# Shifted low weight words in a PSUM tile among the up-projection's banks

## The chip, the cores and the metric

The kernel runs on one core of one Trainium2 chip. A core has five engines that work side by side: TensorE (PE; its weight loads are shown apart, as PEld), VectorE (DVE), ScalarE (ACT), GpSimd (POOL) and SyncE (SP, which here only issues transfers). SBUF is the working memory of all engines, PSUM the memory that PE writes and that DVE and ACT read and write; the kernel's operations on POOL all have their operands in SBUF. The metric is the device time of one execution in microseconds (us), the median of several runs.

## What is computed

A banded attention over 8 batches, 8 heads, 576 positions and 64 elements a head (each position sees itself and the 127 before it, with a slope per head on the distance), and after it a feed-forward network on the 4608 rows of 512 values:

```python
scores = scale * np.matmul(q, k.transpose(0, 1, 3, 2))
mask = (rel >= 0) & (rel < window)
scores = np.where(mask, scores + bias[None], -1000000000.0)
attn = softmax(scores); attn_out = np.matmul(attn, v)
x = attn_out.transpose(0, 2, 1, 3).reshape(B * S, H * D)
h = x @ w_in                                   # 512 x 2048
g = h * (1.0 / (1.0 + np.exp(-1.702 * h)))
out = (g @ w_out).astype(np.float32)           # 2048 x 512
```

The softmax is written short here. The two weight matrices reach the kernel as 64-bit words: two 32-bit words for each value, the low one first. The kernel makes fp32 values of them itself; that is the decoding that the change is about.

## The kernel before, in words

The rows of the network are worked in 18 chunks of T = 256, the hidden width in 16 slices of 128. For a chunk and a slice f, `Job.up(f)` (line 576) makes h in a PSUM tile of tag `h_ps` with 12 matmuls (the weight and the input each as a high and a low part, three products, four pieces of 128); ACT takes a tanh of it (line 585), DVE makes the gelu g from it (line 586, which reads h from PSUM too), ACT casts its high part (589) and POOL subtracts for the low part (590). `Job.down(f)` (line 593) adds 6 matmuls into two PSUM accumulators. The main loop (from line 930) emits `up` of the next step ahead of `down` of the present one. The last six chunks go in pairs, with other code (`Pair`, from 685), when all the weights have long been decoded.

Attention goes in units through a pipeline of stages, one `tick` (line 819) at a time: loads, scores on PE (line 342 in the first two batches, 352 later), bias and minimum on DVE (369), exponents on ACT (392), normalising on POOL, ACT and DVE (417, 420), transposes on PE (438), their copies (446), and the product with v (495). The first seven ticks or so run ahead of the network, with dummy matmuls between them (`spin`, 203); from then on `advance` spreads the ticks over the steps of the network.

Weights come as 32 halves, `w1` and `w2` of each of the 16 slices. `fetch` loads one as 512 64-bit words per partition into a tile of 4 KB (the loads are kept in order on SP's queue). `decode` (line 219) makes of it a high and a low fp32 part, in the same 4 KB:

- line 227, ACT: the top words, scaled, into a tile `wc` of tag `o`, of which there are five; the attention's `xb`, the network's outputs and `half`, and the tiles of `sums` use the same five.
- line 228, DVE: the low words shifted right by 29, in place.
- line 229, DVE: `wc` shifted left by 3, or-ed with those bits, into `wc`.
- line 232, ACT: the high part, a cast of `wc`; line 233, POOL: the low part, a subtraction.

`decode_next` (857) decodes the next half. Three halves are decoded during the first ticks, five at the first step of the network, about two a step until slice 7 is done, then about one a step. The first eight are pinned behind what stands ahead of them on their engine; the rest aren't. For slices from 8 on the `w1` half's `wc` is kept until its neighbour is decoded too; then `sums` (650) makes sums and differences of the pair (DVE, lines 654 to 657), casts and subtracts them (660, 661; the casts go to tiles `wh` of tag `o`) and sends them to DRAM for the paired chunks at the end (664, 665).

The order of the instructions on each engine is laid out once, when the program is built: a scheduler goes through a timeline of its own, gives each engine the first instruction in program order whose inputs are ready, and hands out a tag's buffers as tiles are first written; a buffer comes free when all readers of its tile are done. On the chip each engine then keeps this order, and waits where an input or a buffer comes later than the timeline had it. PSUM has eight banks: two for `h_ps`, one each for `s_ps` and `x_ps`, two for `t_ps` and two for the accumulators. In the first ticks the attention's products `x_ps` of the first four units also use the tag `h_ps`.

Of the kernel before, what the change touches and what calls it, by code (L numbers as in the profile page):

```python
# [11 lines left out]
I32 = mybir.dt.int32  # L12
I64 = mybir.dt.int64
AF = mybir.ActivationFunctionType
ALU = mybir.AluOpType
# [5 lines left out]
P = 128  # L21
# [132 lines left out]
def tile_kernel(ctx: ExitStack, tc: tile.TileContext, q0, k0, v0, qT, kT, v, w_in, w_out, out):  # L154
    nc = tc.nc
# [6 lines left out]
    ps = ctx.enter_context(tc.tile_pool(name="ps", bufs=1, space=PSUM))  # L162
# [56 lines left out]
    def decode(st, name, pin=lambda ins: ins):  # L219

        words = st.bitcast(I32).rearrange("p (m two) -> p m two", two=2)
        top, low = words[..., 1], words[..., 0]
        c = ffn.tile([P, 512], I32, name="wc", tag="o", bufs=OBUFS)

        pin(nc.scalar.activation(c.bitcast(F32), top.bitcast(F32), AF.Prelu, scale=2.0 ** -112, alpha=2.0 ** 32))
        pin(nc.vector.tensor_scalar(low, low, 29, None, ALU.logical_shift_right))
        pin(nc.vector.scalar_tensor_tensor(c, c, 3, low, ALU.logical_shift_left, ALU.bitwise_or))
        w = c.bitcast(F32)  # L230
        res = const.tile([P, 2, 512], F32R, name=name, tag=name)
        pin(nc.scalar.copy(res[:, 0], w))
        pin(nc.gpsimd.tensor_tensor(res[:, 1], w, res[:, 0].bitcast(F32), ALU.subtract))
        if name.startswith("w1"):
            kept[name] = w
        return res
# [620 lines left out]
    def decode_next():  # L857
        nonlocal halves
        g, ws = halves // 2, (w1, w2)[halves % 2]

        pin = [tc.keep_in_program_order] if halves < PINNED else []
        ws[g] = decode(ws[g], f"w{1 + halves % 2}_{g}", *pin)
        halves += 1
        if ws is w1 and g >= F0 and g % 2:
            sums(g // 2, kept.pop(f"w1_{g - 1}"), kept.pop(f"w1_{g}"))
# [175 lines left out]
```

## Time and profile before

| | |
|---|---|
| median of 3 runs | 1059.15 us (1058.39 to 1060.15) |
| profiled execution | 1062.32 us, span 1060.5 us |
| mean granted TensorE clock | 0.988 |
| busy share PE / PEld / DVE / ACT / POOL | 98% / 86% / 64% / 64% / 58% |
| decoding, POOL subtraction (line 233) | 32 times, 1251 ns at least, 1282 in the middle, 3418 at most |
| decoding, ACT top words (227) and cast (232) | 32 times each, 676 and 620 ns in the middle |

The profile is one execution, taken by the hardware profiler; the span runs from the first instruction to the last, and the profiled execution's own time has a little more around it. A row of a group gives line, engine, operation, the tiles written and read, the count, the busy time, the mean of one, and the idle time of the engine just before, with who ended it. A row of the timeline gives start, duration, engine, line, operation, tiles and count, and in brackets the idle time before it and its releaser. A row of the table of stages gives the stretch, its length, the busy time and count of each engine (or of one line alone), the granted clock as a share of full speed, the share of the transfer engines, and GB/s.

### The profile page before, as it was taken

The page shows a single profiled execution, that of the slowest core. Times are in us where ns is not written, and L with a number is a line of the kernel's source. Part 1 is how long each engine was busy: PE and PEld are TensorE (multiplying, and loading weights), DVE is VectorE, ACT ScalarE, POOL GpSimd, SP SyncE. Part 2 cuts the span into 40 slices and gives each one's busy share as a digit, 9 for nine tenths or more (in the row PEclk, how much of TensorE's full clock was granted, in tenths as well). Part 3 has the DMA queues.
Part 4 walks back from the last instruction along what each step waited for, and adds up shares of the span by engine and source line. Part 5 has one row for each costly group of instructions (what it writes and reads, how often), then busy time and mean ns, then how long its engine had stood idle before and what let it go on. Part 6 is the DMA issues. An engine that isn't in the chain of part 4 may idle for free.

```text
span 1060.5 us, 21877 instructions
## 1 busy us (share of the span) xinstructions
PE 1037.9 (98%) x6897; PEld 913.6 (86%) x6897; DVE 683.0 (64%) x2280; ACT 675.4 (64%) x1974; POOL 620.1 (58%) x832
## 2 busy tenths in 40 slices
PE   8889999999999999999999999999999999999998
PEld 5557878789998999999899999999988998898987
DVE  6877576357777787867778686776744345436343
ACT  6968876568777777777777777777633334335332
POOL 3668887457676677767677676766642233215121
PEclk9969999999999999999999999999999999999999
DMA  8975456333224234332423432342174556556551
GB/s 286 371 239 185 147 160 196 108 85 94 80 83 131 82 96 125 112 80 89 141 83 113 119 107 81 106 136 69 57 274 163 170 174 212 179 165 205 188 179 60
DMA packets 120276, 151.91 MB, mean 143 GB/s; under 512 B 40033, under 2 KB 96865, under 8 KB 120161
## 3 DMA queue, kind: packets, MB, share of 16 engines
q1 hardware_dynamic: 114400, 140.55, 42.6%
q10 hardware_dynamic: 5760, 9.96, 2.6%
q8 instruction: 55, 0.90, 0.4%
q14 instruction: 61, 0.49, 0.2%
HBM read 119.01 MB, written 31.46 MB: 142 GB/s over the span
## 4 chain that ended last, share of the span: by engine, by line
PE 79%; DVE 4%; issue 1%; DMA 1%; ACT 1%; POOL 0%; POOLq 0%; ACTq 0%; SPq 0%; DVEq 0%
PE acc L600 21%; PE h_ps L580 21%; PE accs L780 11%; PE X_ps L721 6%; PE s_ps L352 5%; PE x_ps L518 4%; PE Y_ps L721 4%; PE t_ps L461 4%; PE x_ps L495 1%; DVE xf L710 0%; DMA xf<-x 0%; PE t_ps L438 0%; DVE xh L564 0%; DMA part<-wc 0%; DVE xl L566 0%
## 5 line engine op out<-in xcount | busy, mean ns | idle before, releaser
L580 PE MATMUL h_ps<-xh,w 128*128 128x256 f32 x1536 | 251.5, 288 | 8.4 <-DVE g L586 7.5
L580 PEld LDWEIGHTS h_ps<-xh,w 128*128 128x128 f32 x1536 | 213.4, 190 | 26.9 <-issue 7.5
L600 PE MATMUL acc<-w,gh 128*128 128x512 f32 x768 | 220.8, 402 | 0.5 <-ACT g L585 0.4
L590 POOL TENSOR_TENSOR gl<-g,gh 128x256 fp32r<-128x256 f32 x192 | 147.1, 767 | 99.4 <-ACT gh L589 78.0
L733 POOL TENSOR_TENSOR gs<-g,gs 128x512 fp32r<-128x512 f32 x48 | 63.4, 1320 | 168.7 <-PE Y_ps L721 113.8
L780 PE MATMUL accs<-w,gs 128*128 128x512 f32 x576 | 148.3, 393 | 0.3 <-POOL gs L733 0.3
L600 PEld LDWEIGHTS acc<-w,gh 128*128 128x128 f32 x768 | 131.7, 190 | 18.2 <-ACT g L585 0.8
L330 POOL TENSOR_TENSOR K<-rk,K 128x384 fp32r<-128x384 f32 (+1 forms) x120 | 108.8, 907 | 50.7 <-ACT K L328 45.5
L580 PE MATMUL h_ps<-xl,w 128*128 128x256 f32 x768 | 137.2, 284 | 0.2 <-DVE xl L566 0.2
L600 PE MATMUL acc<-w,gl 128*128 128x512 f32 x384 | 127.3, 407 | 1.1 <-POOL gl L590 1.1
L780 PEld LDWEIGHTS accs<-w,gs 128*128 128x128 f32 x576 | 102.2, 189 | 17.7 <-POOL gs L733 0.7
L580 PEld LDWEIGHTS h_ps<-xl,w 128*128 128x128 f32 x768 | 112.4, 191 | 5.2 <-issue 0.6
L399 ACT ACTIVATE pb<-pb,mins 128x256 f32<-128x256 f32 (+2 forms) x216 | 104.6, 486 | 11.6 <-DVE mins L380 11.1
L586 DVE SCALAR_TENSOR_TENSOR g<-g,h_ps 128x256 f32<-128x256 f32 x192 | 79.5, 415 | 49.6 <-ACT g L585 48.1
L589 ACT CAST gh<-g 128x256 fp32r<-128x256 f32 x192 | 77.6, 405 | 50.2 <-DVE g L586 45.4
L585 ACT ACTIVATE g<-h_ps 128x256 f32<-128x256 f32 x192 | 72.7, 380 | 56.1 <-PE h_ps L580 45.9
L380 DVE CUSTOM_DVE_ANT_0 pb<-s_ps,bias 128x256 f32<-128x256 f32 (+3 forms) x240 | 86.0, 380 | 26.9 <-PE s_ps L352 24.7
L424 DVE TENSOR_SCALAR_CACHE_REDUCE pb<-pb,rec 128x256 f32<-128x256 f32 (+2 forms) x216 | 91.0, 454 | 3.2
L329 POOL TENSOR_TENSOR Q<-rq,Q 64x256 fp32r<-64x256 f32 (+1 forms) x120 | 83.0, 691 | 13.6 <-ACT Q L310 3.4
L480 DVE TENSOR_TENSOR pl<-t_ps,ph 128x512 fp32r<-128x512 f32 (+2 forms) x120 | 72.9, 607 | 16.0 <-ACT ph L474 14.1
L461 PE MATMUL t_ps<-ident,pb 128*128 128x128 f32 x408 | 80.8, 272 | 0.5 <-DVE pl L480 0.5
L328 ACT CAST K<-rk 128x384 fp32r<-128x384 f32 (+1 forms) x120 | 56.5, 471 | 29.4 <-PE s_ps L352 23.7
(116 smaller groups left out, 2057.8 us busy)
## 6 DMA issues: line engine op xcount, KB each, us to landing
ring<-part SPq DMA_DIRECT2D x84, 512.0 KB, 3.3
rk<-kT SPq DMA_DIRECT2D x72, 192.0 KB, 2.6
rq<-qT SPq DMA_DIRECT2D x96, 128.0 KB, 2.4
out<-o ACTq DMA_DIRECT2D x34, 256.0 KB, 2.8
rw<-w_in SPq DMA_DIRECT2D x16, 512.0 KB, 6.0
rw<-w_out SPq DMA_DIRECT2D x16, 512.0 KB, 6.8
x<-xf SPq DMA_DIRECT2D x13, 512.0 KB, 3.4
xf<-x SPq DMA_DIRECT2D x13, 512.0 KB, 4.4
```

The lines of the kernel that those rows point to most:

```text
L329: nc.gpsimd.tensor_tensor(Q[D:], rq[D:], Q[D:].bitcast(F32), ALU.subtract)
L330: nc.gpsimd.tensor_tensor(K2, rk, K1.bitcast(F32), ALU.subtract)
L380: nc.vector.tensor_tensor_reduce(b.p[ra:rb, cs:b.end], u.s[ra:rb, e, cs:b.end], bias[head][ra:rb, cs:b.end], -SCALE, BIG, ALU.add, ALU.min ...
L399: nc.scalar.activation(live, live, AF.Exp, bias=u.mins[:b.rows, e:e + 1], scale=-1.0, accum_out=u.sums[:b.rows, e, :1],)
L424: nc.vector.tensor_scalar(live, live, u.rec[:rows, e:e + 1], None, ALU.mult, ALU.add, u.rec[:rows, 2 + e:3 + e])
L461: nc.tensor.transpose(u.t[:c.n, w:w + b.rows], b.p[:b.rows, col:col + c.n], ident[:b.rows, :b.rows])
L580: nc.tensor.matmul(h, w1[f][:, z, k * P:(k + 1) * P], x[:, k], start=(n == 0), stop=(n == len(ops) - 1))
L586: nc.vector.scalar_tensor_tensor(g, g, 1.0, h, ALU.add, ALU.mult)
L590: nc.gpsimd.tensor_tensor(gl, g, gh.bitcast(F32), ALU.subtract)
L600: products.append(nc.tensor.matmul(acc, g[:, t * P:(t + 1) * P], w2[f][:, z], start=(f == self.f0 and n == 0), stop=(f == self.f1 - 1 and ...
L721: nc.tensor.matmul(bank, w[:, z, k * P:(k + 1) * P], x[:, y, k], start=start and i == 0, stop=i == len(ops) - 1, skip_group_check=True)
L780: products.append(nc.tensor.matmul(self.acc[t], g[:, y, t * P:(t + 1) * P], w2[f][:, z], start=(f == 0 and n == 0), stop=(f == NF - 1 and ...
```

## The change

The shifted low words no longer go back into the weight's own tile. A PSUM tile `bits` of one bank is taken for each decoding from the tag `h_ps`, whose two banks the up-projection uses; the shift writes there, and the shift-and-or reads its second operand from there. Nothing else is edited.

```diff
         pin(nc.scalar.activation(c.bitcast(F32), top.bitcast(F32), AF.Prelu, scale=2.0 ** -112, alpha=2.0 ** 32))
-        pin(nc.vector.tensor_scalar(low, low, 29, None, ALU.logical_shift_right))
-        pin(nc.vector.scalar_tensor_tensor(c, c, 3, low, ALU.logical_shift_left, ALU.bitwise_or))
+        bits = ps.tile([P, 512], I32, name="bits", tag="h_ps", bufs=2)
+        pin(nc.vector.tensor_scalar(bits, low, 29, None, ALU.logical_shift_right))
+        pin(nc.vector.scalar_tensor_tensor(c, c, 3, bits, ALU.logical_shift_left, ALU.bitwise_or))
         w = c.bitcast(F32)
```

## The prediction

> **What bounds the kernel now.** I read the page first, then the table of stages, the chain of waits of the early stage, and its timeline instruction by instruction.
>
> ```profile
> span 1060.5 us, 21877 instructions
> PE 1037.9 (98%) x6897; PEld 913.6 (86%) x6897; DVE 683.0 (64%) x2280; ACT 675.4 (64%) x1974; POOL 620.1 (58%) x832
> ```
>
> The span is 1060.5 us; the profiled execution took 1062.32, so 1.82 lie around it, and it is 3.17 above the median of 1059.15. PE is the bound of the whole, but an average says nothing about a change to 32 decodings that all run early. When they run, and when their two DVE steps run, is in the rows of the two lines, first by duration, then split at 57 us:
>
> ```profile
> L228 DVE TENSOR_SCALAR rw<-rw x32: 399/427/5895, 19.4 to 95.8; 128x512 int32<-128x512 int32 x32
> L229 DVE SCALAR_TENSOR_TENSOR wc<-wc,rw x32: 674/692/2507, 21.8 to 150.6; 128x512 int32<-128x512 int32 x32
> 15.00:57.00 42.00, 12.83 (x20) 0.92 1.02 362
> 15.00:57.00 42.00, 7.32 (x8) 0.92 1.02 362
> ```
>
> The last two are the shift (L228) and the shift-and-or (L229), in that order. Two things are to be seen. The shift runs far ahead of its partner: 20 against 8 by 57 us, and the last at 95.8 against 150.6. It can, because it writes into the weight's own tile and takes no buffer. And both have a long tail: 427 ns in the middle but 5895 at worst. So the stage that matters is 20 to 157 us, here in five pieces:
>
> ```profile
> 40.00:48.60 8.60, 6.88 (x45) 4.50 (x43) 8.57 (x23) 8.05 (x24) 5.95 (x6) 1.00 1.05 378
> ...
> 57.00:63.00 6.00, 6.00 (x44) 4.40 (x42) 5.75 (x11) 5.43 (x14) 5.23 (x4) 1.00 0.87 275
> 63.00:68.00 5.00, 0.01 (x1) 0.00 (x0) 5.00 (x3) 0.07 (x1) 4.28 (x4) 0.81 0.79 268
> 68.00:79.60 11.60, 11.56 (x48) 8.27 (x48) 6.34 (x20) 7.63 (x23) 5.60 (x5) 0.50 0.58 169
> 100.00:157.00 57.00, 55.75 (x353) 45.09 (x352) 36.69 (x86) 43.77 (x121) 49.66 (x45) 1.00 0.48 154
> ```
>
> The columns after the length are PE, PEld, DVE, ACT and POOL, then the granted clock. From 63 to 68 PE does nothing, and for the next 11.6 us its clock is 0.50. From 100 us on PE is busy 55.75 of 57 us. So what PE loses before 100 us is lost for the whole, and so is any gap that the change tears into the later stretch. The stop at 63 us:
>
> ```profile
> PE h_ps L580 <- DVE g L586: 6.5, 3, 5.0
> 61.67 5.89 DVE L228 TENSOR_SCALAR rw<-rw 128x512 int32<-128x512 int32 x1
> 62.35 4.92 POOL L233 TENSOR_TENSOR w<-wc,w 128x512 fp32r<-128x512 f32 x4
> 67.48 0.41 DVE L586 SCALAR_TENSOR_TENSOR g<-g,h_ps 128x256 f32<-128x256 f32 x1
> 68.04 1.20 PE L580 MATMUL h_ps<-xh,w 128*128 128x256 f32 x4 [5.03 <-DVE g L586]
> ```
>
> A shift that takes 0.43 us elsewhere sits on DVE for 5.89, exactly while POOL does four subtractions in a row; behind it waits the gelu's L586, and PE cannot start the next up-projection, since L586 still reads the bank of `h_ps` that it needs. Note the last point: **the up-projection already waits for its two banks**.
>
> **The change, part by part.** *The shift's own cost.* It reads SBUF as before and writes PSUM. No row shows that form; the nearest are the shift itself and a one-input DVE operation of the same size that reads PSUM; for operands that change sides there is one line in three forms:
>
> ```profile
> L627 DVE TENSOR_SCALAR o<-acc 128x512 f32<-128x512 f32 x18 | 11.8, 683 | 0.9 <-PE acc L600 0.8
> L728 DVE SCALAR_TENSOR_TENSOR g<-g,p 128x256 f32<-128x256 f32 x24 | 24.8, 1031 | 12.3 <-ACT g L727 12.3
> L728 DVE SCALAR_TENSOR_TENSOR g<-g,X_ps 128x256 f32<-128x256 f32 x24 | 10.1, 421 | 37.1 <-ACT g L727 37.1
> L228 DVE TENSOR_SCALAR rw<-rw 128x512 int32<-128x512 int32 x32 | 30.3, 963 | 4.1 <-DMA rw<-w_in 4.1
> L229 DVE SCALAR_TENSOR_TENSOR wc<-wc,rw 128x512 int32<-128x512 int32 x32 | 28.3, 895 | 6.2 <-ACT wc L227 6.0
> ```
>
> Bounds 427 and 683 ns; I take 683, the row with a PSUM operand: 32 x 0.683 = 21.9 us on DVE in place of 30.3, since the mean of 963 goes. *The shift-and-or* now has one input in PSUM. L728 does the same work with its second input in SBUF (1031 ns) and in PSUM (421 ns); so I take 692 ns, its own middle, for all 32: 22.1 in place of 28.3. Together DVE is spared 8.4 + 6.2 = 14.6 us. DVE is not the bound on average, so that is worth only what PE waits for, which is the stop above: 5.0 us idle, and at most 11.6 x 0.50 = 5.8 us of slow clock behind it. Bounds -5.0 and -10.8. Of the clock I take half, as PE waits for decoded weights there too: **-7.9 us**. The same work could be freed before 57 us; I count none.
>
> Here a page speaks, too. The Trainium skill, "SBUF — State Buffer", section "Who interferes with whom", says that a DVE instruction with at most one SBUF input and outside the two-port modes does not contend with GpSimd. The two L728 rows agree for the two-input form; no run here shows it for a shift that writes PSUM. By that rule alone the change is a pure gain, which is the first rival below; the sum goes by the rows.
>
> *What the change adds.* The bits take a bank of tag `h_ps`, of which there are two, and hold it from the shift to the shift-and-or. Nothing else in the decoding moves. But every order on an engine is laid out when the program is built, taking what is ready, and the shift was ready long before its partner (20 against 8). So I expect it still to run as soon as a bank is free, and then hold that bank until the partner's other input is there. That input (L227) needs one of five buffers of tag `o`. From weight 8 on, two of them keep a pair's `w1` words for `sums`, two are the `wh` of `sums`, and so the shift-and-ors come in bursts with long gaps:
>
> ```profile
> 87.50 1.52 DVE L229 SCALAR_TENSOR_TENSOR wc<-wc,rw 128x512 int32<-128x512 int32 x1
> 103.96 0.69 DVE L229 SCALAR_TENSOR_TENSOR wc<-wc,rw 128x512 int32<-128x512 int32 x1 [0.66 <-ACT wc L227]
> 106.31 1.29 DVE L229 SCALAR_TENSOR_TENSOR wc<-wc,rw 128x512 int32<-128x512 int32 x2
> 117.92 0.84 DVE L229 SCALAR_TENSOR_TENSOR wc<-wc,rw 128x512 int32<-128x512 int32 x1 [1.24 <-ACT wc L227]
> 123.69 1.11 DVE L229 SCALAR_TENSOR_TENSOR wc<-wc,rw 128x512 int32<-128x512 int32 x1
> 134.76 0.87 DVE L229 SCALAR_TENSOR_TENSOR wc<-wc,rw 128x512 int32<-128x512 int32 x1 [1.31 <-ACT wc L227]
> 141.02 1.10 DVE L229 SCALAR_TENSOR_TENSOR wc<-wc,rw 128x512 int32<-128x512 int32 x1
> 150.63 0.86 DVE L229 SCALAR_TENSOR_TENSOR wc<-wc,rw 128x512 int32<-128x512 int32 x1 [1.32 <-ACT wc L227]
> ```
>
> From the end of one row to the start of the next burst: 14.9, 10.3, 10.0 and 8.5, together 43.7 us in which the next weight's bits can sit in a bank. Then one bank is left for the up-projections, and each must wait until the gelu of the one before has read it. The cycle on one bank, from rows inside a gap and outside:
>
> ```profile
> 107.84 1.20 PE L580 MATMUL h_ps<-xh,w 128*128 128x256 f32 x8
> 108.87 0.62 PE L580 MATMUL h_ps<-xl,w 128*128 128x256 f32 x4
> 113.65 0.42 DVE L586 SCALAR_TENSOR_TENSOR g<-g,h_ps 128x256 f32<-128x256 f32 x1
> 120.29 0.28 PE L580 MATMUL h_ps<-xl,w 128*128 128x256 f32 x1
> 121.03 0.42 DVE L586 SCALAR_TENSOR_TENSOR g<-g,h_ps 128x256 f32<-128x256 f32 x1 [0.32 <-ACT g L585]
> 100.00:157.00 57.00, 5.60 (x14) 1.00 0.48 154
> ```
>
> The up-projection takes 107.84 to 109.49, 1.65 us, and its gelu is done at 114.07, 4.58 later: 6.2 us a cycle. Outside the gap the gelu ends 0.88 us behind (120.57 to 121.45): 2.5 a cycle. The last row counts 14 gelus in 57 us, one in 4.07. So an up-projection on one bank costs PE between nothing and 2.1 us; I take 1.3, nearer the row that lies in a gap. In 43.7 us there are 43.7 / 4.07 = 10.7 of them: **+13.9 us** (0 to 22.5). Before 57 us the shifts take banks too, but PE is busy only 6.88 of 8.60 us there (the row from 40 us) and has the attention's matmuls to fill a wait with; I count nothing, and 6 us if that cover is gone (four up-projections end before 68 us, at 1.5 each, between the 0 and the 2.1 above). Behind a PE that waits there, the attention's matmuls queue as well, since the order on PE is fixed when the program is built; the shift itself sits on DVE behind the gelu that frees its bank and waits for nothing new. DMAs, ACT and POOL get no instruction more or less.
>
> Sum: 1062.32 - 7.9 + 13.9 = 1068.3 for a profiled execution like this one, and 3.17 less on the median's scale: **1065**.
>
> **The rivals.** *Pure gain.* The shift runs just before its partner, holds the bank about 1.4 us (0.683 + 0.692), and only the relief is left: 1059.15 - 7.9 = 1051 (1048 to 1054). For it: the relief can be read from the rows; against it: 20 shifts against 8. It decides from about 6 banked up-projections downward (7.9 / 1.3). Chance 0.36.
>
> *Both banks taken.* In a gap the next two weights' bits hold both, and no up-projection runs. A step's PE work:
>
> ```profile
> 721.90 1.40 PE acc L600 x6
> 739.07 1.41 PE h_ps L580 x12
> ```
>
> That is 2.8 us; 14 of them (2.81 each) leave 55.75 - 39.3 = 16.4 of 57 us for the rest, 0.29 a us. In a gap of 10.9 us PE has two down-projections (2.8) and 3.2 us of the rest, and idles 4.9: 19.6 over four, less 7.9, makes 1071; if the clock then halves twice as it did at 68 us (5.8 each), 1082. For it: DVE idles in the gaps, so it takes a bank the moment one is free; against: an up-projection stands earlier in the program than a far weight's shift. Chance 0.14.
>
> *No difference.* Relief and banks cancel within 2 us, or the stop at 63 us only moves to another DVE instruction with two SBUF inputs: 1059. Chance 0.12.
>
> **How the numbers follow.** The forecast has 0.38, both banks 0.14, together 0.52 for slower; faster 0.36; same 0.12. About 0.2% (2 us) is what a measurement can tell here. The range 1049 to 1082 takes in the gain short of its far end, and the loss up to both banks with a halved clock; within the forecast alone it would be 1062 to 1074 (10.8 off and 13.9 on, to 7.9 off and 22.5 on).
>
> **What would show it.** Right: L228 has no tail, middle near 683 ns, and lies close before L229, at most two ahead; L229 stays at 692 with no tail; no PE stop of 5 us behind a shift; in its place PE's L580 waits for L229 or L586 between 87 and 151 us, and PE has fewer than 55.75 busy us of the 57. Wrong: L228 far ahead still and no wait at L580 (then a bank isn't held, and the pure gain is right), or L228 with its tail (then it wasn't its place of writing that let POOL stop it).

## The result and the profile after

The changed kernel takes 1050.4 us (median of four runs, 1050.24 to 1053.46) where the kernel before takes 1059.19 (1058.39 to 1060.15): a ratio of 0.992, with an interval of 0.990 to 0.994. It became faster by 8.8 us, where the prediction forecast 1065 and had 1051 for its first rival, the pure gain. In the changed kernel the lines behind the edit are numbered one higher: the shift is L229, the shift-and-or L230, POOL's subtraction L234, the up-projection L581, its gelu L587, the down-projection L601.

The head of the page after, and the rows of the two edited lines and of POOL's subtraction by duration (minimum, middle, maximum in ns, first and last start in us):

```profile
span 1048.4 us, 21904 instructions
PE 1031.3 (98%) x6897; PEld 908.1 (87%) x6897; DVE 671.8 (64%) x2280; ACT 675.5 (64%) x1974; POOL 608.8 (58%) x832
```

```profile
L229 DVE TENSOR_SCALAR bits<-rw x32: 677/694/706, 18.8 to 128.3; 128x512 int32<-128x512 int32 x32
L230 DVE SCALAR_TENSOR_TENSOR wc<-wc,bits x32: 658/686/691, 21.2 to 133.7; 128x512 int32<-128x512 int32 x32
L234 POOL TENSOR_TENSOR w<-wc,w x32: 1263/1285/1467, 22.7 to 136.3; 128x512 fp32r<-128x512 f32 x32
```

Both tails are gone: the longest shift takes 706 ns where it took 5895, the longest shift-and-or 691 where it took 2507. The shift in its middle costs 694 ns in place of 427, as the row with a PSUM operand had it. POOL gains too: its longest subtraction takes 1467 ns, where it took 3418. And the last shift starts 5.4 us ahead of the last shift-and-or, not 55.

The table of stages after (length, then PE, PEld, DVE, ACT, POOL busy with counts, granted clock). The first two rows are the shift and the shift-and-or alone up to 57 us; the next are four of the five pieces that the prediction shows, and then the long stretches:

```profile
15.00:57.00 42.00, 8.27 (x12) 0.92 1.02 365
15.00:57.00 42.00, 7.54 (x12) 0.92 1.02 365
```

```profile
40.00:48.60 8.60, 5.27 (x24) 3.00 (x22) 5.27 (x16) 7.92 (x24) 6.38 (x6) 0.73 1.03 365
63.00:68.00 5.00, 5.00 (x40) 4.10 (x39) 4.19 (x9) 4.94 (x16) 5.00 (x6) 1.00 1.01 363
68.00:79.60 11.60, 11.60 (x76) 8.73 (x75) 7.96 (x28) 9.85 (x37) 9.40 (x11) 1.00 1.02 352
100.00:157.00 57.00, 56.90 (x367) 45.56 (x366) 40.38 (x97) 42.08 (x118) 40.81 (x41) 1.00 0.46 148
15.00:57.00 42.00, 37.26 (x245) 24.61 (x243) 31.02 (x103) 38.60 (x115) 25.60 (x27) 0.92 1.02 365
57.00:100.00 43.00, 42.11 (x283) 32.44 (x280) 32.45 (x94) 39.42 (x126) 36.73 (x39) 1.00 0.79 266
157.00:1047.00 890.00, 883.82 (x5939) 798.48 (x5938) 560.66 (x1948) 547.75 (x1595) 501.29 (x713) 1.00 0.41 127
```

The same long stretches of the kernel before (its row from 100 us stands in the prediction):

```profile
15.00:57.00 42.00, 38.87 (x239) 25.31 (x235) 33.84 (x104) 35.94 (x107) 24.80 (x25) 0.92 1.02 362
57.00:100.00 43.00, 36.50 (x218) 27.50 (x216) 34.05 (x70) 28.57 (x90) 32.34 (x29) 0.84 0.63 205
157.00:1047.00 890.00, 885.94 (x5981) 800.93 (x5980) 567.15 (x1977) 555.62 (x1626) 506.39 (x720) 1.00 0.42 128
```

Four things are to be seen. Up to 57 us shift and partner now stand 12 to 12. From 63 to 68 us, where PE did nothing, it is busy without a gap, and the 11.6 us behind it run at clock 1.00 and not 0.50. Not all is better: from 40 to 48.6 us PE is less busy than before (5.27 us for 6.88, at clock 0.73 for 1.00). And the whole gain is made by 157 us: PE has by then begun 245 + 283 + 367 = 895 matmuls since 15 us, where it had begun 239 + 218 + 353 = 810. After 157 us one takes 885.94 / 5981 = 0.148 us of PE on average, so the 85 that are ahead are worth some 12.6 us, an estimate, as matmuls differ in size. The two spans differ by 12.1; the medians differ by less, 8.8, because the execution that was profiled before lies 3.17 us above its median. Of the 85, 65 are gained between 57 and 100 us, 14 in the stretch behind, where the prediction saw its loss.

What PE waited for between 15 and 160 us in the changed kernel (idle us in total, times, the longest):

```profile
PE s_ps L343 <- DMA rk<-k: 1.9, 1, 1.9
...
PE h_ps L581 <- DVE wc L230: 0.8, 1, 0.8
...
PE h_ps L581 <- DVE g L587: 0.4, 1, 0.4
```

The up-projection stood 0.8 us for the shift-and-or (between 51 and 57 us) and 0.4 for a gelu (between 57 and 87): 1.2 us, against 13.9 in the prediction. The wait of 1.9 us, in front of a score matmul at 45.8 us, is put down to a transfer; the weight loads of the same matmuls are put down to a shift (L229), so the bits may have a part in it, and with all of it the waits would be 3.1 us.

### The profile page after: what moved, and what is told of

Its sections match the earlier page's. It is cut to its first block, busy times and chain, and to the rows that moved or that the text cites. A ratio compares the mean times of both kernels' runs of the same rounds, so it can differ in the third digit from the quotient of the medians.

```text
span 1048.4 us, 21904 instructions
## 1 busy us (share of the span) xinstructions
PE 1031.3 (98%) x6897; PEld 908.1 (87%) x6897; DVE 671.8 (64%) x2280; ACT 675.5 (64%) x1974; POOL 608.8 (58%) x832
## 4 chain that ended last, share of the span: by engine, by line
PE 88%; DVE 4%; DMA 3%; ACT 2%; issue 2%; POOL 1%; SPq 0%; POOLq 0%; ACTq 0%; DVEq 0%
PE h_ps L581 24%; PE acc L601 24%; PE accs L781 11%; PE X_ps L722 6%; PE s_ps L353 5%; PE x_ps L519 4%; PE Y_ps L722 4%; PE t_ps L462 4%; PE x_ps L496 2%; DMA rw<-w_out 2%; PE t_ps L439 1%; PE s_ps L343 1%; PE sb_ps L343 1%; DVE xh L565 1%; ACT pb L393 1%
## 5 line engine op out<-in xcount | busy, mean ns | idle before, releaser
L581 PE MATMUL h_ps<-xh,w 128*128 128x256 f32 x1536 | 247.0, 287 | 2.4 <-DVE g L587 1.3
L581 PEld LDWEIGHTS h_ps<-xh,w 128*128 128x128 f32 x1536 | 212.1, 189 | 19.5 <-DVE g L587 2.8
L601 PE MATMUL acc<-w,gh 128*128 128x512 f32 x768 | 218.6, 400 | 0.0
L591 POOL TENSOR_TENSOR gl<-g,gh 128x256 fp32r<-128x256 f32 x192 | 143.4, 747 | 106.2 <-ACT gh L590 74.3
L601 PEld LDWEIGHTS acc<-w,gh 128*128 128x128 f32 x768 | 130.4, 188 | 17.4 <-ACT pw L447 0.3
L581 PE MATMUL h_ps<-xl,w 128*128 128x256 f32 x768 | 135.2, 282 | 0.2 <-DVE xl L567 0.2
L601 PE MATMUL acc<-w,gl 128*128 128x512 f32 x384 | 125.9, 406 | 0.0
L581 PEld LDWEIGHTS h_ps<-xl,w 128*128 128x128 f32 x768 | 110.6, 188 | 4.7 <-DVE xl L567 0.4
L587 DVE SCALAR_TENSOR_TENSOR g<-g,h_ps 128x256 f32<-128x256 f32 x192 | 79.8, 415 | 53.7 <-ACT g L586 51.5
L590 ACT CAST gh<-g 128x256 fp32r<-128x256 f32 x192 | 77.7, 405 | 48.6 <-DVE g L587 43.1
L330 POOL TENSOR_TENSOR Q<-rq,Q 64x256 fp32r<-64x256 f32 (+1 forms) x120 | 83.9, 699 | 12.6 <-ACT Q L311 3.2
L353 PE MATMUL s_ps<-K,Q 128*128 128x256 f32 (+1 forms) x432 | 75.6, 286 | 0.0
```

The costliest lines, as they stand in the source:

```text
L330: nc.gpsimd.tensor_tensor(Q[D:], rq[D:], Q[D:].bitcast(F32), ALU.subtract)
L353: nc.tensor.matmul(u.s[:b.rows, e, b.first:b.end], u.Q[:, b.q0 - u.q0:b.q0 - u.q0 + b.rows], k[:, ko:ko + b.end - b.first], start=(z == 0) ...
L581: nc.tensor.matmul(h, w1[f][:, z, k * P:(k + 1) * P], x[:, k], start=(n == 0), stop=(n == len(ops) - 1))
L591: nc.gpsimd.tensor_tensor(gl, g, gh.bitcast(F32), ALU.subtract)
L601: products.append(nc.tensor.matmul(acc, g[:, t * P:(t + 1) * P], w2[f][:, z], start=(f == self.f0 and n == 0), stop=(f == self.f1 - 1 and ...
```

## The experiments

Two theories were to be told apart at first. By the first, the gain comes from **the operands**: with an operand in PSUM, neither step is held up by POOL any more. By the second it comes from **the order**: the banks hold the shift back, from 20 against 8 to 12 against 12, so the scheduler lays out another order on every engine, and that happens to be a better one. A third question was why the bank cost next to nothing.

### The order of the changed kernel with the old operands

```diff
+        traced = [i for i in nc.cur_bb.bb.instructions if "Boundary" not in type(i).__name__]
+        if order:
+            for line in order.values():
+                for a, b in zip(line, line[1:]):
+                    tc.add_manual_dep(
+                        traced[b], traced[a].name,
+                        mybir.DependencyInfo(mybir.DependencyClass.NoSync, mybir.DependencyReason.DATA),
+                        reason="same_order")
...
+    order = build(plan, arrays, "psum")
...
-    build(nc, arrays)
+    build(nc, arrays, "sbuf", order)
```

The program is built twice. The first time it is the changed kernel, of which only the order on each engine is kept. The second time (the form "sbuf") the decoding is that of before, in place; but each instruction is tied behind the one that stands ahead of it on its engine in the changed kernel, with an edge that orders and does not wait; so every engine has the changed kernel's order, instruction by instruction. The helper code moves the lines: the shift is L234, the shift-and-or L235, POOL's subtraction L244.

> The decoding of before (shift in place, both inputs of the shift-and-or in SBUF), but with every engine's order of instructions taken from the changed kernel, instruction by instruction. Theory P (the gain is that POOL no longer stops the two DVE steps): about 1058 us or more, with the tails back (shift up to several us). Theory O (the gain is the new order alone): 1050 us within 1.5. Theory B (the bits' hold on the banks costs something that a relief outweighs) adds: PE's waits for the banks behind the shift-and-or are gone, 1 to 3 us in favour of this kernel.

It took 1059.35 us (1058.04 to 1061.92, twelve runs), a ratio to before of 0.9998 (0.9984 to 1.0012). Its two rows by duration, and its stages:

```profile
L234 DVE TENSOR_SCALAR rw<-rw x32: 409/629/3419, 18.8 to 135.3; 128x512 int32<-128x512 int32 x32
L235 DVE SCALAR_TENSOR_TENSOR wc<-wc,rw x32: 678/702/3554, 21.2 to 140.9; 128x512 int32<-128x512 int32 x32
```

```profile
15.00:57.00 42.00, 38.30 (x249) 25.20 (x248) 32.98 (x100) 39.20 (x117) 27.92 (x27) 0.92 1.03 370
57.00:100.00 43.00, 38.42 (x240) 29.03 (x239) 38.38 (x83) 34.12 (x107) 35.81 (x34) 0.96 0.71 242
100.00:157.00 57.00, 55.56 (x350) 44.48 (x349) 41.10 (x95) 41.84 (x117) 49.47 (x43) 1.00 0.48 152
```

The tails are back, on both steps, and with them the time: 249 + 240 + 350 = 839 matmuls by 157 us, 56 fewer than in the changed kernel. 56 x 0.148 is 8.3 us; the two medians are 8.95 apart, and the order is the same. So the gain comes with the two steps' operands, less what their banks cost, and the new order by itself is worth nothing (1059.35 for 1059.32 of the kernel before beside it): the second theory falls. How a tail comes about is in the timeline of this kernel around 66 us:

```profile
65.26 1.10 POOL L431 TENSOR_SCALAR pb<-pb,rec 64x192 f32<-64x192 f32 x1 [1.59 <-DVE rec L422]
65.85 3.55 DVE L235 SCALAR_TENSOR_TENSOR wc<-wc,rw 128x512 int32<-128x512 int32 x1
66.33 2.51 POOL L244 TENSOR_TENSOR w<-wc,w 128x512 fp32r<-128x512 f32 x2
68.82 1.18 POOL L601 TENSOR_TENSOR gl<-g,gh 128x256 fp32r<-128x256 f32 x1
```

And the same place of the changed kernel:

```profile
66.69 0.69 DVE L230 SCALAR_TENSOR_TENSOR wc<-wc,bits 128x512 int32<-128x512 int32 x1
66.95 2.52 POOL L234 TENSOR_TENSOR w<-wc,w 128x512 fp32r<-128x512 f32 x2
```

With both inputs in SBUF the shift-and-or sits on DVE for 3.55 us, while POOL goes through the rest of one instruction, two whole subtractions and the start of a fourth with hardly a gap; with one in PSUM it takes its 0.69 and ends while POOL is still in the first of the same two subtractions. All the steps of these kernels say the same. In the kernel before and in this one, none of the 28 steps that overlap no POOL instruction takes longer than 431 ns (shift) or 707 (shift-and-or), and all 51 that take longer than 750 ns overlap one. In the changed kernel 57 of the 64 overlap one, and none takes longer than 706. The Trainium skill, "SBUF — State Buffer", section "Who interferes with whom", says that an instruction on VectorE that reads at most one input from SBUF, outside the two-port modes, doesn't contend with GpSimd. The 64 steps of the changed kernel agree, 706 ns at most, the shift that writes PSUM among them. The in-place shift reads only one input from SBUF too and is held all the same (3419 ns); whether it runs in a two-port mode, no row here shows.

### Half of the weights

The same tied order; the 16 halves of `w1` are decoded as in the changed kernel, the 16 of `w2` in place.

```diff
-        if form == "psum":
+        if form == "psum" or form == "half" and name.startswith("w1"):
```

> The changed kernel's order again, instruction by instruction; the w1 halves use PSUM as in the changed kernel, the w2 halves are decoded in place as before. If the whole gain is POOL's stops of the two DVE steps (theory P), half of them bring about half of it: 1053 to 1057 us. If single long stops decide, it may fall on either end (1050 or 1059).

It took 1054.09 us (1052.95 to 1054.92, six runs), a ratio of 0.9942 (0.9927 to 0.9956): 5.4 of some 9 us. Its rows side by side (busy us, mean ns, idle before):

```profile
L234 DVE TENSOR_SCALAR rw<-rw 128x512 int32<-128x512 int32 x16 | 12.1, 758 | 0.0
L235 DVE SCALAR_TENSOR_TENSOR wc<-wc,rw 128x512 int32<-128x512 int32 x16 | 19.6, 1224 | 6.5 <-ACT wc L233 5.8
L230 DVE TENSOR_SCALAR bits<-rw 128x512 int32<-128x512 int32 x16 | 11.0, 690 | 0.3
L231 DVE SCALAR_TENSOR_TENSOR wc<-wc,bits 128x512 int32<-128x512 int32 x16 | 10.9, 684 | 0.7
```

In one execution the 16 in-place pairs cost DVE 31.7 us, the 16 pairs through PSUM 21.9. With 0, 16 and 32 decodings freed in the same order the kernel takes 1059.35, 1054.09 and 1050.40 us: the gain goes with their number, which is what the first theory says. The halves of `w2` alone were not tried.

### The order alone, another way

The kernel before, with each shift tied behind the last half's shift-and-or, so that it can't run far ahead.

```diff
-        pin(nc.vector.tensor_scalar(low, low, 29, None, ALU.logical_shift_right))
-        pin(nc.vector.scalar_tensor_tensor(c, c, 3, low, ALU.logical_shift_left, ALU.bitwise_or))
+        shift = pin(nc.vector.tensor_scalar(low, low, 29, None, ALU.logical_shift_right))
+        if ors:
+            tc.add_manual_dep(
+                shift.ins, ors[-1].ins.name,
+                mybir.DependencyInfo(mybir.DependencyClass.NoSync, mybir.DependencyReason.DATA),
+                reason="behind_the_or")
+        ors.append(pin(nc.vector.scalar_tensor_tensor(c, c, 3, low, ALU.logical_shift_left, ALU.bitwise_or)))
```

> The kernel before, with each shift only ordered behind the shift-and-or of the half before it, so that shifts and shift-and-ors alternate as in the changed kernel, by an order of the scheduler's own and without any bank. Theory P: 1057 to 1062 us, tails as before. Theory O: 1049 to 1053 us.

1063.33 us (1062.65 to 1063.92, five runs), a ratio of 1.0041 (1.0027 to 1.0054). That is 1.3 us beyond the range of the first theory and 10 beyond that of the second. Keeping the shift close doesn't help. The scheduler laid out a third order here, and 4 us are lost in it. Its steps are held by POOL more than before (67.6 us of DVE for 58.6), so part of the loss may be that. Still, an edit that only lets the scheduler find another order moves this kernel by about half of what was being looked for, and so only the kernels with a tied order can be read to a few us.

### A shift that comes late

The changed kernel, with the shift waiting for its partner's other input (L227), so that the bank is held as briefly as can be.

```diff
-        pin(nc.scalar.activation(c.bitcast(F32), top.bitcast(F32), AF.Prelu, scale=2.0 ** -112, alpha=2.0 ** 32))
+        first = pin(nc.scalar.activation(c.bitcast(F32), top.bitcast(F32), AF.Prelu, scale=2.0 ** -112, alpha=2.0 ** 32))
         bits = ps.tile([P, 512], I32, name="bits", tag="h_ps", bufs=2)
-        pin(nc.vector.tensor_scalar(bits, low, 29, None, ALU.logical_shift_right))
+        shift = pin(nc.vector.tensor_scalar(bits, low, 29, None, ALU.logical_shift_right))
+        tc.add_manual_dep(
+            shift.ins, first.ins.name,
+            mybir.DependencyInfo(mybir.DependencyClass.Sync, mybir.DependencyReason.DATA),
+            reason="late_shift")
```

> The changed kernel, with each shift made to wait for the top words of its half (line 227), so that a bank is held for about 1.4 us and no longer. If holding a bank costs something (theory B): 1047 to 1049 us. If it costs nothing: 1050.4 us within 2, what the changed order alone may move.

1056.09 us (1054.86 to 1057.81, eleven runs), a ratio of 0.9974 (0.9965 to 0.9982): faster than before, but 5.7 us slower than the changed kernel, and outside both of the ranges expected. So there is no sign that holding the bank kept the changed kernel from more. DVE stood 9.8 us for L227 in front of the shift, and the order is its own; which of the two costs the 5.7 us stays open.

### The other operand in PSUM

The kernel before, but ACT puts the top words in a bank of `h_ps`; the shift stays in place, with all its operands in SBUF, and the shift-and-or has one input in PSUM.

```diff
-        pin(nc.scalar.activation(c.bitcast(F32), top.bitcast(F32), AF.Prelu, scale=2.0 ** -112, alpha=2.0 ** 32))
+        t = ps.tile([P, 512], I32, name="top", tag="h_ps", bufs=2)
+        pin(nc.scalar.activation(t.bitcast(F32), top.bitcast(F32), AF.Prelu, scale=2.0 ** -112, alpha=2.0 ** 32))
         pin(nc.vector.tensor_scalar(low, low, 29, None, ALU.logical_shift_right))
-        pin(nc.vector.scalar_tensor_tensor(c, c, 3, low, ALU.logical_shift_left, ALU.bitwise_or))
+        pin(nc.vector.scalar_tensor_tensor(c, t, 3, low, ALU.logical_shift_left, ALU.bitwise_or))
```

> The other operand in PSUM: the top words go to a bank of h_ps, the shift is in place again and can run ahead, the shift-and-or has one SBUF input as in the changed kernel. Theory P, if the shift's stops are what cost: 1056 to 1061 us, with a tail on the shift and none on the shift-and-or; if the shift-and-or's stops are what cost: 1050 to 1053. Theory O: about 1059, as the shift runs ahead again.

1055.28 us (1052.25 to 1056.75, seven runs), a ratio of 0.9962 (0.9948 to 0.9976). The shift-and-or lost its tail (687 ns in the mean) and the shift kept a short one (1665 at most). It lies between the ranges expected for the two steps. It is half the gain, in an order of its own, and an order alone can do as much; how the gain divides between the two steps is not settled by it. It was not tried with the tied order.

### One bank taken for good, old decoding

Now the price of a bank. The kernel before, with a small tile that takes one of the two banks of `h_ps` from the first chunk's start until the last half is decoded; the two lines that fill and read it add nothing to the computation.

```diff
     begin(jobs[0])
+    held = ps.tile([P, 1], F32, name="held", tag="h_ps", bufs=2)
+    tc.keep_in_program_order(nc.vector.memset(held, 0.0))
...
                 decode_next()
+            if halves == 2 * NF:
+                nc.vector.tensor_tensor(
+                    const.tile([P, 1], F32, name="sink"), held, w2[NF - 1][:, 1, :1].bitcast(F32), ALU.add)
```

> The kernel before (in place, no bits), with a tile of one column that holds one of the two h_ps banks from the network's first step until the last half is decoded, so that every up-projection of the stage runs on one bank. My prediction's price (1.3 us for each such up-projection, some 22 of them) gives 1059 + 28 = 1087 us. Theory B0 (other work of PE fills the wait, a bank costs nearly nothing): 1059 within 5, which is what the order alone may move.

1069.86 us (1067.71 to 1074.23, six runs), a ratio of 1.0092 (1.0072 to 1.0112): 10.4 us more than the 1059.5 beside it, between the 1087 of the prediction's price and the 1059 within 5 of a price of nothing. The up-projection's matmuls from 15 to 160 us, PE's waits for the gelu that frees the bank in that stretch, and the table of stages:

```profile
15.00:160.00 145.00, 42.82 (x288) 0.96 0.70 238
```

```profile
PE h_ps L580 <- DVE g L586: 7.0, 6, 4.5
```

```profile
15.00:57.00 42.00, 37.26 (x238) 24.39 (x235) 33.92 (x105) 35.18 (x101) 24.62 (x24) 0.96 1.01 367
57.00:100.00 43.00, 35.29 (x221) 26.47 (x222) 34.62 (x81) 32.72 (x108) 36.89 (x32) 0.92 0.65 217
100.00:157.00 57.00, 53.49 (x337) 41.53 (x336) 36.05 (x85) 45.26 (x120) 48.22 (x42) 1.00 0.52 163
```

288 matmuls are 24 up-projections. If the whole loss were the bank's, one that has a single bank would cost 10.4 / 24 = 0.43 us, a third of the 1.3 taken in the prediction. The order is this kernel's own, though, so that 4 us more or less may be the order's: with 4 us more it would be 0.6, still under half of 1.3. And only a small part of the loss is made while the bank is held (it is free again at 153 us). By 157 us PE has begun 238 + 221 + 337 = 796 matmuls, 14 fewer than before: some 2.1 us at 0.148, or 0.1 us an up-projection, an estimate. From 157 to 1047 us it begins 37 fewer (5944 for 5981) with both banks free. Nor do the waits grow much: the kernel before, with both banks, shows 6.5 us of the same wait, and the longest here (4.5 us) ends with a gelu that came right behind a shift-and-or of 3.44 us beside POOL. Most of the 24 do not wait at all: PE stood six times.

### One bank taken for good, new decoding

The same held tile in the changed kernel: bits and up-projections share the one bank that is left. The added lines are those above.

> The changed kernel with the same column tile, so that bits and up-projections of the stage share one single bank. The prediction's price: 1050 + 28 or more, 1080 to 1090 us, as no up-projection runs while bits wait for their top words. Theory B0: 1050 to 1060.

1100.86 us (1098.68 to 1103.14, four runs), a ratio of 1.0383 (1.0361 to 1.0404): 50 us more than the changed kernel, beyond every figure expected. PE's waits from 15 to 160 us, and its stretch from 100 us:

```profile
PE acc L601 <- ACT gh L590: 16.5, 10, 3.0
PE h_ps L581 <- DVE wc L230: 4.1, 3, 1.9
```

```profile
100.00:157.00 57.00, 40.78 (x237) 31.08 (x235) 28.10 (x70) 35.69 (x90) 31.00 (x30) 0.93 0.38 120
```

Here PE is busy 40.78 of 57 us, and begins 237 matmuls where the changed kernel begins 367. An up-projection on the one bank now waits for a shift-and-or, and the down-projections wait for the casts of late gelus. These two rows are 20.6 of the 50 us; the rest was not taken apart. So the mechanism of the prediction exists; here it took a second holder, on the other bank, to show.

### The bits among other banks

The changed kernel, with the bits in the two banks of `t_ps`, which the attention's transposes use.

```diff
-        bits = ps.tile([P, 512], I32, name="bits", tag="h_ps", bufs=2)
+        bits = ps.tile([P, 512], I32, name="bits", tag="t_ps", bufs=2)
```

> The changed kernel with the bits among the two banks of t_ps (attention's transposes) and not of h_ps. Theory P: the gain stays, 1048 to 1056 us with the order's own scatter of some 5, both steps without a tail. If the choice of h_ps mattered, PE would wait at the transposes (line 439) instead, and the gain would be gone (1059).

1062.13 us (1059.81 to 1066.21, twelve runs), a ratio of 1.0021 (1.0005 to 1.0038). The rows of the two steps:

```profile
L229 DVE TENSOR_SCALAR bits<-rw 128x512 int32<-128x512 int32 x32 | 21.8, 688 | 6.6 <-ACT pw L447 6.4
L230 DVE SCALAR_TENSOR_TENSOR wc<-wc,bits 128x512 int32<-128x512 int32 x32 | 21.8, 683 | 13.3 <-ACT wc L227 12.9
```

No tail, and yet no gain; the 1048 to 1056 us that the first theory expected are missed. PE's waits at the transposes for the shift-and-or are 0.2 us, so it isn't the other expected cause either. DVE stands 6.4 us for the copies that empty the transposes' banks, and 12.9 for L227, where it stood 5.4 in the changed kernel. The last shift-and-or starts at 149.4 us, not at 133.7. That the freed steps alone don't make the gain is shown; whether the waits or this kernel's own order took it back is not.

## Why the prediction was wrong

**The relief was right in kind, and its size in part by luck.** The prediction had 7.9 us for the stops that go, between 5.0 and 10.8. With the order the same, the two forms lie 8.95 us apart, which is the relief less what the banks cost. The two steps became what it took them for: 694 and 686 ns in the middle, no tail, for 683 and 692. And the stop at 63 us is gone, with the slow clock behind it. But the prediction took all of its 7.9 us from that one stop, in one execution with a granted clock of 0.988. Of the 41 runs of the kernel before that were timed beside the experiments, those within 1 us of 1059.2 have 0.993 to 0.997, and the five above 1062 us have 0.987 to 0.990; so the slow clock that it priced may be larger there than in most. And with the changed kernel's order and the old operands there is no 5 us stop, yet 57 to 100 us still loses 42.11 - 38.42 = 3.7 us of PE's time and some of its clock (0.96), and the stretch behind 56.90 - 55.56 = 1.3 us more. Such stops, spread over several places, cost about the same as the one; nothing in the prediction's working gave that.

**The step that failed is the bank's price**, "In 43.7 us there are 43.7 / 4.07 = 10.7 of them: +13.9 us". It failed in both factors.

*How long the bits sit.* "I expect it still to run as soon as a bank is free, and then hold that bank until the partner's other input is there." It doesn't run that soon. The shifts and their partners alternate strictly, and between the bursts the next shift mostly comes late, as these rows of the changed kernel show. A hold lasts from a shift to the end of the shift-and-or behind it:

```profile
102.19 0.69 DVE L229 TENSOR_SCALAR bits<-rw 128x512 int32<-128x512 int32 x1
103.48 0.68 DVE L230 SCALAR_TENSOR_TENSOR wc<-wc,bits 128x512 int32<-128x512 int32 x1
107.73 0.69 DVE L229 TENSOR_SCALAR bits<-rw 128x512 int32<-128x512 int32 x1
...
110.29 0.69 DVE L230 SCALAR_TENSOR_TENSOR wc<-wc,bits 128x512 int32<-128x512 int32 x1
115.82 0.69 DVE L229 TENSOR_SCALAR bits<-rw 128x512 int32<-128x512 int32 x1
```

From 104.16 to 107.73 and from 110.98 to 115.82 no bits sit in a bank, though the words were there: the last load of a half was issued at 70.5 us, and the loads take 6.5 to 7.0 us in the middle to land. The rule that the prediction named against its own rival, that an up-projection stands earlier in the program than a far weight's shift, would explain why; that was argued, and no run tests it. After 80 us only five of the 13 holds are longer than 2 us, 24.5 us together (7.6, 3.9, 4.2, 2.8 and 6.0), not 43.7. Long holds are thickest where the prediction counted nothing: before 51 us eight in a row last 3.0 to 5.7 us each, and the only wait of PE there in which the bits may have a part is the 1.9 us at 45.8 us.

*What a hold costs.* 1.3 us an up-projection was taken between nothing and 2.1, from one row in a gap where a gelu came 4.58 us late. With a bank gone for the whole stage the price is 0.43 if the whole loss is put down to it, and some 0.1 by what is lost in the stage, and in the changed kernel PE's waits at the up-projection come to 1.2 us for all holds together. The timeline of the longest hold of 100 to 157 us shows what PE does meanwhile:

```profile
128.33 0.68 DVE L229 TENSOR_SCALAR bits<-rw 128x512 int32<-128x512 int32 x1
129.46 1.18 PE L581 MATMUL h_ps<-xh,w 128*128 128x256 f32 x8
130.48 0.62 PE L581 MATMUL h_ps<-xl,w 128*128 128x256 f32 x4
131.56 0.59 PE L343 MATMUL sb_ps<-rk,rq 64*128 64x256 f32 x2
132.08 0.74 PE L601 MATMUL acc<-w,gl 128*128 128x512 f32 x2
132.79 1.18 PE L601 MATMUL acc<-w,gh 128*128 128x512 f32 x4
133.66 0.68 DVE L230 SCALAR_TENSOR_TENSOR wc<-wc,bits 128x512 int32<-128x512 int32 x1
134.49 1.10 PE L581 MATMUL h_ps<-xh,w 128*128 128x256 f32 x8
```

While the bits hold one bank, an up-projection runs in the other, and until its gelu has read that one, PE has scores and a down-projection to do. The prediction named this cover for the time before 57 us and left it out behind, where it is there too: PE is busy 56.90 of the 57 us from 100 us on.

**The rivals.** The pure gain came to pass at 1050.4 for 1051, with a chance of 0.36; the hold it supposed (1.4 us) is near the 1.4 to 2.0 us of eight of the 13, but not of the longer ones, which cost little all the same. Its point of decision, six banked up-projections, was worked out with the wrong price: at 0.43 it takes 7.9 / 0.43 = 18 to lose the relief. Both banks taken by bits never happened, since a second shift never runs ahead. "No difference" was wrong in its second form too: the stop didn't move to another instruction.

**What was to show it.** Right were the shift without its tail, near 683 ns, at most two ahead (it is one); the shift-and-or at 692 without its tail; and no stop of 5 us. Wrong were the waits of L580 between 87 and 151 us (PE has none for L230 or L587 there; the 1.2 us lie before) and fewer than 55.75 busy us in the 57: there are 56.90. "At most two ahead" could not tell the forecast from the pure gain, since two is all that the tag's two banks allow.

**What stays open**: how the 8.95 us divide between shift and shift-and-or, what one bank less costs in an order that is the same, and why the late shift and the `t_ps` banks lose what they lose.

## What to carry to other kernels

Where a DVE instruction with all its operands in SBUF has a long tail beside busy POOL work, moving one operand to PSUM can pay even if its middle gets slower (427 to 694 ns here), provided a bank is left for the others. Price a shared bank by what the bound engine can do in the meantime, not by the cycle of the one who must wait: two banks of which one is often taken cost 1.2 us of PE's waits here, one bank for both some 50 us of the kernel's time. And where a change lets a scheduler lay out a new order, tie the order of one variant to the other's before a difference of a few us is given a cause.

## What the runs showed that was not expected

A DVE instruction can be held through several POOL instructions in a row, not only through the one that it met: the shift-and-or of 3.55 us above ends only after two whole subtractions that began behind it. With the changed kernel's order the in-place steps are held more often than in the kernel before: 30 of the 64 take longer than 750 ns, for 21, and they cost 28.9 + 33.3 = 62.2 us of DVE, for 30.3 + 28.3 = 58.6; yet the two kernels take the same time. In the changed kernel the two steps take 44.0 us. And a small edit that only ties the shift (the order alone, another way) moved the time by 4 us, through the order that the scheduler made of it.
